# A spectral filter and a gated FFN on one core: inverse column transforms as five 64-row pairs, and an FFN begun on two of four token tiles

## The chip, the cores and the metric

The kernel runs on one core of a Trainium2 chip. A core has a matrix engine (PE, with its weight loads shown apart as PEld), VectorE (DVE), ScalarE (ACT), GpSimd (POOL) and SyncE (SP), which here only issues DMAs. Each engine works off its own queue in order; they meet through semaphores. The metric is device time in microseconds for one execution, as the median of several runs. The profile is of one further execution and has its own time.

## The reference

```python
def _A_ref(x, w_r, w_i):
    X = jnp.fft.rfft2(x.astype(jnp.float32), axes=(-2, -1))
    X = X * (w_r + 1j * w_i)
    return jnp.fft.irfft2(X, s=(S, D), axes=(-2, -1)).astype(jnp.bfloat16)

def _B_ref(x, w_gate, w_up, w_down):
    return (gelu(x @ w_gate) * (x @ w_up)) @ w_down

h   = x + _A_ref(layernorm(x), w_r, w_i)
out = h + _B_ref(layernorm(h), w_gate, w_up, w_down)
```

S is 2048 tokens, D is 576, the FFN is F = 4608 wide; inputs are bfloat16. A is a two-dimensional Fourier transform over tokens and features, a product with a complex weight, and the inverse. B is a feed-forward block with a gate (Gelu by the tanh formula).

## The kernel before, in words

The Fourier transforms are matmuls with tables of sines and cosines that the kernel makes itself. A token index is split into 16 x 128, so that a transform over tokens is one of length 16 (F16, `row16`, line 288) followed by one of length 128 with twiddles in the tables TF (forward) and TI (inverse, TF turned by a DMA transpose, `turn_tf`, line 261). The feature transform uses the table DT (three blocks of 128 features), with DF, DI and DS as rearranged pieces of it: DI and DS are filled by six small DMAs (lines 413 to 421). Only J = 289 of the 576 feature frequencies are kept.

The middle part (lines 646 to 685) is a hand-made pipeline over eight column groups, in the order 1, 2, ..., 7, 0. For group k:

- `f2` (line 471): 6 matmuls per column, two columns (k and k + 8), 290 wide; the result `pq` is copied from PSUM by ACT (VectorE for column 9).
- `f3` (line 496): two halves of 4 matmuls; ACT copies the results `g` and `hs`.
- `sums_of` (line 520): VectorE forms `xab` from g and hs, two operations.
- `wmul` (line 526): VectorE multiplies with the filter's parts (WR, WI; `m1`, `m2`), forms `za`, `zb`, and writes the two halves of Zt (lines 552 and 553). That makes eight VectorE operations a group with the two of the next group's `sums_of`, which stand between zb and Zt. Group 0 is written in two pieces of its columns.
- `i3` (line 557): the inverse of the length-128 transform, 10 matmuls 256 wide (24 of 128 for group 0), in three steps spread between other matmuls; ACT copies the results into EO.

Three Zt buffers go round. `weights()` (line 451) writes the negated second half of WI and halves the first and last column of WR and WI, on VectorE, before the first group's multiplication.

Then come the inverse column transforms, `inv_cols(x, g)` (line 613), for two halves x of the groups and eight g of 256 tokens: six matmuls of 128 rows, 290 wide, three for the even and three for the odd frequencies, each half into a PSUM bank of its own. ACT copies the result (scaled) to `cw` or `cs`. `add_rows` and `add_sum` (lines 731 and 782) do the length-16 inverse on PE and add the result to h, with the sum over features; ACT forms the sum of squares, `head_rstd` (line 792) makes mean and 1/deviation on VectorE with a power on POOL.

The normalised rows must lie with features on partitions for the FFN. Two ways: `norm2` writes the row with each 64 features doubled and `flip` turns it by a DMA transpose on SP's queue; `norm_row` and `turn` let PE turn it (18 transposes of 64 columns) and VectorE or ACT copy it. Of the first four token tiles 0 and 1 go by DMA and 2 and 3 by PE. The order of this head is written out by hand in lines 821 to 847.

The FFN (lines 863 to 929) takes four chunks of 512 tokens. For each of 36 blocks of 128 FFN columns PE does 18 matmuls of 64 rows, 512 wide (line 876): the upper 64 partitions hold the gate's weights, the lower the up-projection's, so that pairs run side by side into two banks. ACT does the Gelu (line 884), VectorE the product (line 885). Weights come in groups of three blocks (`load_gu`, line 141), three buffers. Then W_down: 15 token tiles with pairs of 64 rows (line 897), the last one with 128 rows (line 916). The row sums for later tiles, their norms and flips are put between blocks by the table `todo`. All PSUM tiles of two banks share a ring of four (tag `two`).

Of the kernel before, what the change touches and what calls it, by code (L numbers as in the profile page):

```python
# [32 lines left out]
NJT = 3  # L33
ZS = 320
# [7 lines left out]
def kernel_body(  # L42
# [64 lines left out]
    DI = keep.tile([P, 2, 2, JH], BF16, name="DI")  # L107
    DS = keep.tile([P, 2, 2, JH], BF16, name="DS")
# [54 lines left out]
    Zts = [sp.tile([P, 4, ZS], BF16, name=f"Zt{i}") for i in range(3)]  # L163
# [235 lines left out]
    G.memset(DI[:], 0.0)  # L399
    for z in Zts:  # L400
        G.memset(z[:, :, J:], 0.0)
# [9 lines left out]
    nc.sync.dma_start(WR[:, 9 : H + 1, 0:J], wm[0][:].rearrange("p (r j) -> p r j", r=8))  # L411
    turn_tf(first)
    for dst, src in (
        (DI[64:128, :, 1, :], DT[0:64, 0, :, 1, :]),
        (DI[0 : J - 2 * P, :, 0, :], D3[0 : J - 2 * P, :, 0, :]),
        (DS[0:64, 0, :, :], DT[64:128, 0, :, 1, :]),
        (DS[64:128, 0, :, :], DT[0:64, 1, :, 1, :]),
        (DS[0:64, 1, :, :], DT[64:128, 1, :, 1, :]),
        (DS[64:128, 1, :, :], D3[0:64, :, 1, :]),
    ):  # L420
        nc.sync.dma_start(dst, src)
# [29 lines left out]
    def weights():  # L451
        V.tensor_scalar(WI[:, 9 : H + 1, 0:J], wm[1][:].rearrange("p (r j) -> p r j", r=8), -1.0, None, op0=ALU.mult)
        for w in (WR, WI):
            V.tensor_scalar(w[:, :, 0 : J : J - 1], w[:, :, 0 : J : J - 1], 0.5, None, op0=ALU.mult)
# [5 lines left out]
    pq = {}  # L460
    xab = {}
# [9 lines left out]
    def f2(c):  # L471
# [5 lines left out]
        for par, t in steps:  # L477
# [7 lines left out]
        sb = wk.tile([P, 2, JP], BF16, name="pq", tag="pq", bufs=6)  # L485
        (V.tensor_copy if c == 9 else A.copy)(  # L486
            sb[:].rearrange("p r (j a) -> p r j a", a=2),
            ps[:, :, 0:JP].rearrange("p a (r j) -> p r j a", r=2),
        )
        pq[c] = sb  # L490
# [5 lines left out]
    def f3(k, half):  # L496
# [12 lines left out]
        for r in range(2):  # L509
            if half:  # L510
                comb(ps[:, 1 - r, 0:J], k, C, q[:, r, 0:J], NS, p[:, r, 0:J])
            else:
                comb(ps[:, r, 0:J], k, C, p[:, r, 0:J], SN, q[:, r, 0:J])
# [11 lines left out]

    def wmul(k, i, nxt=None):
        x = xab[k]
        z = Zts[i % 3]
        zt[k] = z
        zv = z[:].rearrange("p (a b) j -> p a b j", a=2)  # L530
        sl = slice(k, 18 - k, 17 - 2 * k) if k else slice(0, 9, 8)
        m1, m2 = (wk.tile([P, 2, 2, JP], BF16, name=n, tag=n, bufs=1) for n in ("m1", "m2"))
        if k:
            za, zb = (wk.tile([P, 2, JP], BF16, name=n, tag=n, bufs=1) for n in ("za", "zb"))
        else:
            za, zb = zv[:, 0], zv[:, 1]

        for j0, j1 in ((0, J),) if k else ((0, P), (P, J)):
            js = slice(j0, j1)
            for w, m in ((WR, m1), (WI, m2)):  # L540
                V.tensor_tensor(
                    m[:, :, :, js],
                    x[:, :, :, js],
                    w[:, sl, js].unsqueeze(1).to_broadcast([P, 2, 2, j1 - j0]),
                    ALU.mult,
                )
            V.tensor_tensor(za[:, :, js], m1[:, 0, :, js], m2[:, 1, :, js], ALU.subtract)
            V.tensor_tensor(zb[:, :, js], m1[:, 1, :, js], m2[:, 0, :, js], ALU.add)
            if nxt:
                sums_of(nxt)  # L550
            if k:
                V.tensor_tensor(zv[:, 0, :, js], za[:, :, js], zb[:, ::-1, js], ALU.add)
                V.tensor_tensor(zv[:, 1, :, js], zb[:, :, js], za[:, ::-1, js], ALU.subtract)
# [3 lines left out]
    def i3(k, s):  # L557
# [3 lines left out]
        z = zt[k][:].rearrange("p c j -> p (c j)")  # L561
# [3 lines left out]
        if k:  # L565
            pv = ps[:].rearrange("p a (n h e l) -> p (a n) e h l", n=2, h=H, l=8)
            for n, w in (((0, 0), (1, 1)), ((2, 3), (3, 4)), ((0, 2),))[s]:
                o = w * P
                T.matmul(pv[:, n], lhsT=z[:, o : o + P], rhs=TI[:, ts[k], 1:3, :], start=True, stop=False)  # L569
                o += 2 * ZS  # L570
                T.matmul(pv[:, n], lhsT=z[:, o : o + P], rhs=TI[:, ts[k], 0:2, :], start=False, stop=True)  # L571
# [13 lines left out]
        for n, c, j, p0, m in (  # L585
            ((0, 0, 0, 0, P), (1, 0, P, 0, P)),
            ((0, 1, 64, 0, P), (1, 1, 192, 0, P)),
            ((0, 0, 256, 0, 64), (0, 1, 0, 64, 64)),
        )[s]:
            for b in range(2):  # L590
                for a in range(2):
                    T.matmul(
                        pv[p0 : p0 + m, n, b],
                        lhsT=z[:, (2 * a + b) * ZS + j : (2 * a + b) * ZS + j + m],
                        rhs=TI[:, ts[8 * b], 1 - a + c, :],
                        start=(a == 0),
                        stop=(a == 1),
                    )
# [14 lines left out]
    def inv_cols(x, g):  # L613

        ps = two("cs_ps")
        for e in range(2):
# [30 lines left out]
    for i in range(n + 1):  # L647
        last = i >= n
        if not last:
            f2(order[i])  # L650
# [325 lines left out]
```

## Time and profile before

| | us |
|---|---|
| median of 3 runs | 502.45 |
| lowest and highest | 502.14, 502.9 |
| the profiled execution, its own time | 502.53 |
| its span in the trace | 500.8 |
| PE busy in the span | 490.8 |

The span runs from the first to the last instruction of the program; the profiled execution's own time has 1.73 us around it. In a group's row the columns are: line, engine, operation, output <- input, shapes, count, then busy time in us, mean ns of one, and the idle time of the engine before them. In a timeline row the columns are start and length in us, engine, line, operation, tiles, shapes, count, and in brackets the idle time before it with what ended it; lengths overlap the next start, so steps are read from start to start. A row of the chain has start, length, engine, tile, line and count. A row of a window has the stretch, its length, the busy time of PE, PEld, DVE, ACT and POOL, the granted PE clock, the DMA share and GB/s. DMA rows end with the size and the time from issue to landing.

### The profile page before, as it was taken

To read this page: it belongs to the slowest core of one execution; us is meant where nothing else is said; L and a number is where in the kernel's file an instruction comes from. 1 tells how busy PE (TensorE), PEld (TensorE's weight loads), DVE (VectorE), ACT (ScalarE), POOL (GpSimd) and SP (SyncE) were. 2 spreads that over 40 slices of the span, in tenths; PEclk is the share of its full clock that TensorE was granted. 3 is DMA by queue.
4 is the path that set the end of the run, shared out by engine and by line. 5 is a ranking of instruction groups with operands and counts; after the bars stand their busy time and mean duration, and the time that the engine had idled before them with its cause. 6 is when DMAs were issued, how large, how long until landed. Compare 5 with 4: busy or idle time off the path is not lost.

```text
span 500.8 us, 12115 instructions
## 1 busy us (share of the span) xinstructions
PE 490.8 (98%) x5418; PEld 316.9 (63%) x5420; DVE 222.9 (45%) x435; ACT 162.3 (32%) x284; POOL 28.5 (6%) x75
## 2 busy tenths in 40 slices
PE   7999999999999999999999999999999999999997
PEld 3467765555569974444499944444799644445995
DVE  8999766788641234433321154333212233333111
ACT  8989973322220112232300123232110223233000
POOL 8500010111110000000000000000000000000000
PEclk9999999999999999999999999999999999999999
DMA  8539686799950029998810099998400497880000
GB/s 282 167 75 200 172 236 160 153 171 193 177 109 3 1 76 192 198 196 156 159 22 1 3 189 189 198 183 156 82 1 3 112 186 154 155 155 1 14 14 24
DMA packets 88114, 61.61 MB, mean 123 GB/s; under 512 B 22781, under 2 KB 86653, under 8 KB 88061
## 3 DMA queue, kind: packets, MB, share of 16 engines
q1 hardware_dynamic: 87773, 59.65, 60.5%
q0 software_dynamic: 288, 1.18, 0.7%
q8 instruction: 42, 0.69, 0.6%
q14 instruction: 11, 0.09, 0.1%
HBM read 52.65 MB, written 2.36 MB: 110 GB/s over the span
## 4 chain that ended last, share of the span: by engine, by line
PE 92%; DVE 3%; ACT 2%; DMA 1%; POOL 1%; issue 0%; POOLq 0%
PE gu L876 56%; PE acc L897 26%; PE pq_ps L478 2%; PE acc L916 2%; PE cs_ps L618 1%; PE f2t L286 1%; PE eo_ps L571 1%; PE y_ps L741 1%; PE eo_ps L569 1%; DMA Bt<-hrow 1%; PE gh_ps L494 1%; ACT Bt L322 1%; DMA h_sb<-in_A_x_dram 1%; DVE h_sb L786 1%; PE gh_ps L493 1%; ACT junk L124 1%
## 5 line engine op out<-in xcount | busy, mean ns | idle before, releaser
L876 PE MATMUL gu<-Bt,wgu 64*128 64x512 bf16 x2592 | 282.2, 376 | 0.9 <-DMA Bt<-hrow 0.9
L876 PEld LDWEIGHTS <-wgu 64*128 64x128 bf16 x2592 | 132.7, 94 | 146.8 <-issue 1.2
L885 DVE TENSOR_TENSOR P_sb<-g_sb,gu 128x512 bf16<-128x512 f32 x144 | 98.7, 685 | 148.8 <-ACT g_sb L884 148.8
L884 ACT ACTIVATE g_sb<-gu 128x512 f32<-128x512 f32 x144 | 86.0, 597 | 196.8 <-PE gu L876 196.8
L897 PEld LDWEIGHTS <-P_sb 64*128 64x128 bf16 x2160 | 130.0, 94 | 3.3
L897 PE MATMUL acc<-wd,P_sb 64*128 64x288 bf16 x1440 | 93.0, 283 | 0.0
L906 DVE TENSOR_TENSOR part<-part,acc 128x576 f32<-128x576 f32 x15 | 11.3, 754 | 111.4 <-ACT part L905 111.4
L905 ACT COPY part<-acc 128x576 f32<-128x576 f32 x15 | 9.6, 638 | 122.5 <-PE acc L897 122.5
L897 PE MATMUL acc<-wd_a,P_sb 64*128 64x288 bf16 x720 | 48.9, 283 | 0.0
L478 PE MATMUL pq_ps<-DT,Bt 128*128 128x290 bf16 x64 | 12.2, 287 | 0.2 <-DVE Bt L328 0.2
L286 PE MATMUL f2t<-h_sb,ident 128*128 128x512 bf16 x26 | 8.8, 494 | 3.7 <-DMA h_sb<-in_A_x_dram 3.7
L766 DVE TENSOR_SCALAR hrow<-h_sb,mv,rstd 128x1152 bf16<-128x1152 bf16 x14 | 12.1, 866 | 0.0
L908 DVE TENSOR_TENSOR h_sb<-h_sb,part 128x576 bf16<-128x576 bf16 x15 | 11.4, 757 | 0.5
L134 POOL TENSOR_TENSOR rstd<-rstd,mhalf 128x1 f32<-128x1 f32 (+1 forms) x16 | 11.2, 699 | 1.3
L618 PEld LDWEIGHTS <-EO 128*128 128x128 bf16 x96 | 9.1, 96 | 3.0 <-issue 0.2
L478 PEld LDWEIGHTS <-Bt 128*128 128x128 bf16 x96 | 9.3, 97 | 2.5 <-issue 0.2
L298 PE MATMUL f2t<-F,xn 128*128 128x256 bf16 x64 | 9.2, 275 | 1.1 <-DVE xn L137 1.0
L133 POOL TENSOR_SCALAR rstd<-mv 128x1 f32<-128x1 f32 (+1 forms) x16 | 3.9, 244 | 107.1 <-DVE mv L119 106.9
L486 ACT CAST pq<-pq_ps 128x580 bf16<-128x580 f32 x15 | 9.8, 662 | 0.4 <-PE pq_ps L478 0.2
L124 ACT ACTIVATE junk<-h_sb 128x576 bf16<-128x576 bf16 x14 | 9.4, 677 | 0.4 <-DMA h_sb<-in_A_x_dram 0.4
L118 DVE BATCH_NORM_STATS2 st<-h_sb 128x6 f32<-128x288 bf16 x21 | 9.3, 442 | 0.0
L117 DVE BATCH_NORM_STATS2 st<-h_sb 128x6 f32<-128x288 bf16 x21 | 9.3, 441 | 0.0
(137 smaller groups left out, 283.5 us busy)
## 6 DMA issues: line engine op xcount, KB each, us to landing
wgu<-in_B_w_gate_dram SPq DMA_DIRECT2D x48, 432.0 KB, 5.3
wgu<-in_B_w_up_dram SPq DMA_DIRECT2D x48, 432.0 KB, 6.9
wd<-in_B_w_down_dram SPq DMA_DIRECT2D x2, 1728.0 KB, 7.7
wd_a<-in_B_w_down_dram SPq DMA_DIRECT2D x1, 1728.0 KB, 15.1
out_dram<-h_sb SPq DMA_DIRECT2D x3, 576.0 KB, 3.9
h_sb<-in_A_x_dram SPq DMA_DIRECT2D x4, 288.0 KB, 3.2
h_sb<-in_A_x_dram SPq DMA_DIRECT2D x2, 576.0 KB, 6.6
WR<-in_A_w_r_dram SPq DMA_DIRECT2D x1, 650.2 KB, 8.8
```

The lines of the kernel that those rows point to most:

```text
L124: A.activation(junk[:], h_sb[:, h, :], fn, scale=sc, accum_out=mv[:, h, i : i + 1])
L134: G.tensor_tensor(dst[:, sl], dst[:, sl], mhalf[:, sl], ALU.pow)
L286: T.matmul(dst, lhsT=ident[:], rhs=h_sb[:, 0, 0:512], start=True, stop=True)
L478: T.matmul(ps[:, par, 0:JP], lhsT=Bt[:, t, col], rhs=DT[:, t // 2, par] if t < 4 else DF[:, par], start=(t == par), stop=(t == 4),)
L618: T.matmul(ps[:, e, 0:JP], lhsT=EO[x][:, 2 * e + jt if jt < 2 else 4, 2 * g : 2 * g + 2].rearrange("p h e k l -> p (h e k l)"), rhs=DI[:, ...
L766: V.tensor_scalar(hrow[:], h_sb[:, h, :].rearrange("p (r k) -> p r k", k=64).unsqueeze(2).to_broadcast([P, NR, 2, 64]), mv2[:, h, 0:1], rs ...
L876: T.matmul(gu[:, c, :], lhsT=w[rows, r, i * P : (i + 1) * P], rhs=hl[tcnk % 2][rows, r, :], start=(r == 0), stop=(r == NR - 1),)
L884: A.activation(g_sb[:], gu[:, 0, :], ACT.Gelu_apprx_tanh)
L885: V.tensor_tensor(p_sb(fa + i), g_sb[:], gu[:, 1, :], ALU.mult)
L897: T.matmul(accs[i][:, c, 0:DH], lhsT=p_sb(f)[rows, st * P : (st + 1) * P], rhs=wd[f // NWA][rows, f % NWA, c * DH : (c + 1) * DH], start=( ...
L906: V.tensor_tensor(part[:], part[:], accs[1][:, :, 0:DH], ALU.add)
L908: V.tensor_tensor(hv, hv, part[:], ALU.add)
```

## The change

Six parts.

1. `inv_cols` takes the 290 frequencies in five blocks of 58 (JW, NW). Even ones lie on partitions 0 to 57, odd ones on 64 to 121, so that ten matmuls of 58 rows make five pairs, one on each half of PE's rows. The table for it is DQ, filled by 13 small DMAs, in place of DI and DS. Zt gets the layout [2, 5, 2, 64] with 58 of 64 used.
2. `f3` gives both outputs of its first half from the first half of pq, and of its second half from the second. Column 9's copy is made in two pieces. The copy of the second group's first column comes after `f3` of the first.
3. WI's second half comes by DMA, without the sign; the halving of two columns is done by POOL; `weights()` is gone. m1 and m2 are allocated once.
4. The second half of Zt is held back and written in the next group's `wmul`, between the second multiplication and za (for the last groups at once). i3's three steps stand together at the end of a turn. Group 0's i3 has 40 matmuls of 64 columns.
5. In the head, tiles 0 and 1 go by PE and tiles 2 and 3 by DMA; VectorE does both copies. Two of the second half's transforms that stood ahead of the FFN stay there, beside the first two; the last four go between FFN blocks.
6. The FFN's first six blocks are done in two sweeps: first for 256 tokens (tiles 0 and 1), with a late transform behind each of the second to the fifth block, then for the other 256. Weight groups are requested when their buffer's last block has been issued. `part` shares a buffer tag with `g_sb`.

```diff
-NJT = 3
-ZS = 320
+JW = 58
+NW = JP // JW
...
+    DQ = keep.tile([P, NW, 2, JH], BF16, name="DQ")
+    Zts = [sp.tile([P, 2, NW, 2, 64], BF16, name=f"Zt{i}") for i in range(3)]
...
-    nc.sync.dma_start(WR[:, 9 : H + 1, 0:J], wm[0][:].rearrange("p (r j) -> p r j", r=8))
+    for w, t in ((WR, wm[0]), (WI, wm[1])):
+        nc.sync.dma_start(w[:, 9 : H + 1, 0:J], t[:].rearrange("p (r j) -> p r j", r=8))
+    for w in (WR, WI):
+        G.tensor_scalar(w[:, :, 0 : J : J - 1], w[:, :, 0 : J : J - 1], 0.5, None, op0=ALU.mult)
     turn_tf(first)
-    for dst, src in (
...
-        nc.sync.dma_start(dst, src)
+    for r in (1, 0):
+        for w in range(1 - r, NW):
+            j0, j1 = w * JW, (w + 1) * JW
+            for lo, hi in ((j0, min(j1, (j0 // P + 1) * P)), ((j0 // P + 1) * P, j1)):
+                if lo < hi:
+                    p0 = 64 * r + lo - j0
+                    nc.sync.dma_start(
+                        DQ[p0 : p0 + hi - lo, w], DT[lo % P : lo % P + hi - lo, lo // P, :, r, :]
+                    )
...
+    m1, m2 = (wk.tile([P, 2, 2, JP], BF16, name=n) for n in ("m1", "m2"))
+    for m in (m1, m2):
+        G.memset(m[:, :, :, J:], 0.0)
...
+        r = half
+        comb(ps[:, r, 0:J], k, C, p[:, r, 0:J], SN, q[:, r, 0:J])
+        comb(ps[:, 1 - r, 0:J], k, C, q[:, r, 0:J], NS, p[:, r, 0:J])
...
         if k:
+            times(WR, m1, slice(0, J))
+            times(WI, m2, slice(0, J))
+            release()
+            za, zb = (wk.tile([P, 2, JP], BF16, name=n, tag=n, bufs=2) for n in ("za", "zb"))
+            parts(za[:], zb[:], slice(0, JP))
             if nxt:
                 sums_of(nxt)
+            V.tensor_tensor(zv[:, :, 0], blocks(za[:]), blocks(zb[:, ::-1]), ALU.add)
+            held.append((zv[:, :, 1], blocks(zb[:]), blocks(za[:, ::-1]), ALU.subtract))
+            if k in order[5:7]:
+                release()
+            return
...
     def inv_cols(x, g):
         ps = two("cs_ps")
-        for e in range(2):
-            for jt in range(NJT):
+        for w in range(NW):
+            for e in range(2):
+                rows = slice(64 * e, 64 * e + JW)
                 T.matmul(
                     ps[:, e, 0:JP],
+                    lhsT=EO[x][rows, w, 2 * g : 2 * g + 2].rearrange("p h e k l -> p (h e k l)"),
+                    rhs=DQ[rows, w] if w or e else DT[rows, 0, :, 0, :],
+                    start=(w == 0),
+                    stop=(w == NW - 1),
                 )
...
-        if last:
-            inv_cols(0, 0)
         if 1 <= i <= n:
             f3(order[i - 1], 0)
-        if i >= 3 and not last:
-            i3(order[i - 3], 0)
...
         if not last and i:
             f2(order[i] + 8)
+            f2_out(order[i] + 8)
         if i >= 3:
-            for jt in range(0 if last else 2, NJT):
-                i3(order[i - 3], jt)
+            for s in range(3):
+                i3(order[i - 3], s)
...
-    for g in (1, 2):
+    for g in (0, 1, 2):
         inv_cols(0, g)
...
     inv_cols(0, 6)
     add_sum(2, y1)
+    inv_cols(0, 7)
     head_rstd(0)
     add_sum(3, y1)
     head_rstd(1)
+    norm_row(0)
+    norm_row(1)
+    inv_cols(1, 2)
+    inv_cols(1, 3)
+    turn(0)
+    turn(1)
     head_rstd(2)
+    norm2(2)
+    flip(2)
     head_rstd(3)
+    norm2(3)
+    flip(3)
     load_wd(2)
...
+    late = [(1, g) for g in range(4, 8)]
+    for f in range(2 * FQ):
+        gate(0, f, groups[f // FQ], f % FQ, 0, 2 * P)
+        if f and late:
+            inv_cols(*late.pop(0))
     for tcnk in range(4):
         for gi in range(NG):
             for i in range(FQ):
+                f = gi * FQ + i
+                gate(tcnk, f, groups[0], i, 2 * P if tcnk == 0 and f < 2 * FQ else 0, 4 * P)
...
+            groups.pop(0)
+            n = tcnk * NG + gi + 3
+            if n < 4 * NG:
+                groups.append(load_gu(n))
```

`gate(tcnk, f, w, i, lo, hi)` is the FFN block of before for the tokens from lo to hi: 18 matmuls hi - lo wide, Gelu, product.

More of the change, by code (lines that the diff above doesn't have):

```diff
@@ L484, in f2, with f2_out @@
             )
[L485 to L488, printed above, removed]
+        pq[c] = wk.tile([P, 2, JP], BF16, name="pq", tag="pq", bufs=6)
+        pq_ps[c] = ps
+    def f2_out(c, copy=A.copy, rs=slice(0, 2)):
+        copy(
+            pq[c][:, rs].rearrange("p r (j a) -> p r j a", a=2),
+            pq_ps[c][:, :, 0:JP].rearrange("p a (r j) -> p r j a", r=2)[:, rs],
         )
-        pq[c] = sb
     def comb(dst, k1, t0, a, t1, b):
@@ L524, in sums_of, with release @@
         V.tensor_tensor(x[:, 1, ::-1, 0:J], g[:, :, 0:J], hs[:, :, 0:J], ALU.add)
+    held = []
+    def release():
+        while held:
+            V.tensor_tensor(*held.pop())
     def wmul(k, i, nxt=None):
@@ L555, in kernel_body @@
+        for w0, w1 in ((0, 2), (2, NW)):
+            lo, hi = w0 * JW, w1 * JW
+            times(WR, m1, slice(lo, min(hi, J)))
+            times(WI, m2, slice(lo, min(hi, J)))
+            V.tensor_tensor(
+                zv[:, 0, :, w0:w1], blocks(m1[:, 0, :, lo:hi]), blocks(m2[:, 1, :, lo:hi]), ALU.subtract
+            )
+            V.tensor_tensor(
+                zv[:, 1, :, w0:w1], blocks(m1[:, 1, :, lo:hi]), blocks(m2[:, 0, :, lo:hi]), ALU.add
+            )
     eo = {}
@@ L788, in add_sum, with sum_squares @@
         )
+        if squares:
+            sum_squares(h)
+    def sum_squares(h):
         junk = roll.tile([P, D], BF16, name="junk", tag="junk", bufs=2)
```

176 lines of the change are left out of this document (63 added, 113 removed).

## The prediction

> **What bounds the kernel now.** I read the page first, then busy time by window, then the chain that ended last.
>
> ```profile
> span 500.8 us, 12115 instructions
> PE 490.8 (98%) x5418; PEld 316.9 (63%) x5420; DVE 222.9 (45%) x435; ACT 162.3 (32%) x284; POOL 28.5 (6%) x75
> PE 92%; DVE 3%; ACT 2%; DMA 1%; POOL 1%; issue 0%; POOLq 0%
> ```
>
> ```profile
> 60.00:80.00 20.00, 19.04 (x204) 12.57 (x202) 11.91 (x36) 13.18 (x26) 2.14 (x4) 1.00 0.75 209
> ```
>
> ```profile
> 50.78 0.74 PE pq_ps L478 x6
> ...
> 52.61 0.12 PE gh_ps L494
> ...
> 53.49 0.11 PE eo_ps L569
> ...
> 57.34 1.49 PE cs_ps L618 x12
> 58.83 1.25 PE eo_ps L592 x24
> ...
> 62.43 1.19 PE y_ps L741 x16
> ...
> 69.50 3.41 DMA Bt<-hrow
> ...
> 73.05 9.89 PE gu L876 x90
> 82.94 0.49 PE y_ps L741 x8
> 83.43 11.65 PE gu L876 x108
> ```
>
> PE is 98% busy, so a gain must come from matmul time removed or from a wait of PE. From 73.05 on PE does nothing but FFN and row sums; the change leaves that stretch alone, except that four transforms enter it. So the whole answer lies before 78.9 us, where three FFN blocks are done (108 matmuls take 11.65, so 54 take 5.83). The chain names the last wait: 3.41 us of DMA transpose ahead of the first FFN block. But window 60 to 80 has PE busy 19.04 of 20: PE has other work there, eight column transforms. Less waiting for the DMA gains only what cannot be refilled.
>
> Ahead of that, the loop over eight column groups is paced by VectorE:
>
> ```profile
> 38.09 0.76 DVE L541 TENSOR_TENSOR m<-xab,WR 128x1156 bf16<-128x1156 bf16 x1
> 38.76 0.76 DVE L541 TENSOR_TENSOR m<-xab,WI 128x1156 bf16<-128x1156 bf16 x1
> 39.56 0.47 DVE L547 TENSOR_TENSOR za<-m,m 128x578 bf16<-128x578 bf16 x1
> ...
> 41.79 0.76 DVE L541 TENSOR_TENSOR m<-xab,WR 128x1156 bf16<-128x1156 bf16 x1
> ...
> 58.48 0.33 DVE L548 TENSOR_TENSOR Zt<-m,m 128x322 bf16<-128x322 bf16 x1
> ```
>
> Same line to same line, 38.09 to 41.79, is 3.70 us. PE's work for one group is 12 f2 matmuls (2 x 0.74), 8 of f3 at 0.12 and 10 of i3 at 0.11: 3.54. VectorE leads by 0.16, no more. Its second multiply starts 0.67 after the first, but L547, which needs that multiply's result, 0.80 after it: 0.13 of dependence.
>
> **Part A: up to the first row sum (before: 63.60).**
>
> Column transforms. Six matmuls of 128 rows cost 0.745 (1.49 for twelve). Ten of 64 rows run as five pairs; eight such matmuls of nearly this width took 0.49 (82.94), so ten take 0.61. That is 0.13 off each of 16, 2.1 in all, but only those on PE's path count. Three lie behind the last Zt write (58.48 + 0.33 = 58.81) and ahead of the row sums at 62.43: 0.4. Those ahead of it only fill time in which PE would otherwise wait for Zt. Those behind the row sums belong to part B.
>
> VectorE's eight operations per group stay, in another order: the held second Zt write now stands between the second multiply and za, and covers the 0.13. It does so in five groups of seven (the first has nothing held, the last nothing either): 0.65. PE's 3.54 lets the period fall just so far. The price is a later second half of Zt: group k's is written in the next group's turn, some 1.7 into it. i3 waits for it, with the next f2 and f3 queued behind it on PE; but i3 has moved to the end of PE's turn, behind 2.5 of f2 and f3, and VectorE wants that f3 a turn later. I cost it at nothing; uncovered, it can take back the 0.16 per group by which VectorE leads.
>
> The Zt writes get 10 runs of 58 elements for 2 of 289. Bounds:
>
> ```profile
> L766 DVE TENSOR_SCALAR hrow<-h_sb,mv,rstd 128x1152 bf16<-128x1152 bf16 x14 | 12.1, 866 | 0.0
> ```
>
> ```profile
> L541 DVE TENSOR_TENSOR m<-xab,WR 128x1156 bf16<-128x1156 bf16 x7 | 5.3, 760 | 0.0
> L541 DVE TENSOR_TENSOR m<-xab,WR 128x512 bf16<-128x512 bf16 x1 | 0.4, 419 | 0.0
> ```
>
> Four runs of 128 cost no more per element than four of 289 (341 ns for 644 more elements): nothing per run. But 18 runs of 64 in L766 took 106 ns more than L541 for the same count: 6 ns a run, 0.06 a write. I take 0.02, nearer the tensor_tensor rows: 14 writes, +0.3 (0 to +0.84).
>
> The first sums may come a little earlier:
>
> ```profile
> 29.13 0.65 ACT L514 CAST hs<-gh_ps 128x578 bf16<-128x578 f32 x1
> ```
>
> They start when this ends, at 29.8. ACT now copies the next group's pq behind g and hs, but f3's first half still needs the same two copies. I take 0.1 (0 to 0.65, one ACT copy). VectorE's `weights` (0.9) falls away ahead of that, where VectorE would wait for hs: nothing. i3 of group 0 becomes 40 matmuls of 64 columns in 20 pairs. Transposes of that width:
>
> ```profile
> 69.77 0.29 PE L618 MATMUL cs_ps<-DI,EO 128*128 128x290 bf16 x1
> 69.98 1.20 PE L811 MATMUL pt<-ident,hflat 128*64 128x128 bf16 x36
> ```
>
> 18 pairs in 1.20, of which 0.2 is the last one's tail: 0.055 a pair, 1.1 for 20, against 1.25 before. I take 0.1. These rows also show a step of 0.21 from a 128 by 128 matmul to a 128 by 64 one, where L618 repeats every 0.12: 0.09 for the change of shape. The Trainium skill ("TensorEngine Tiling (Array Packing)", Key Properties) says that a change of tiling mode drains the engine; the step agrees, and it speaks against this change, since 64-row transforms now stand between 128-row i3. I count seven such changes both before and after: behind the last Zt write two fewer, ahead of it more, where PE waits anyway.
>
> Off the path: SP issues 13 small copies for DQ instead of 6, and WI as a copy; POOL halves two weight columns and waits for that copy.
>
> ```profile
> 12.71 0.96 POOL L381 DMA_INDIRECT wm_i<-in_A_w_i_dram,rev  x1 [0.30 <-issue]
> ```
>
> ```profile
> 26.44 2.60 SPq L421 DMA_DIRECT2D DS<-DT  x4
> ...
> 33.27 3.18 SPq L262 DMA_TRANSPOSE TI<-TF  x1
> ```
>
> ```profile
> WR<-wm_r SPq DMA_DIRECT2D x1, 578.0 KB, 4.5
> wm_i<-in_A_w_i_dram,rev POOLq DMA_INDIRECT x1, 5.7
> ```
>
> WI: 12.71 + 5.7 + 4.5 = 22.9, halved by 24, wanted by VectorE at 30.7 (38.09 less two periods); queued behind it on POOL are only two memsets with the same date. SP: a copy takes 0.65 to issue, and behind the last at 29.04 the queue stood free until 33.27. Seven more end at 33.6, so the second TI transpose, queued behind, starts 0.3 late; its 3.18 end near 36.8, and its tables are first wanted by the third group's i3, near 42. The weight loads behind it are wanted at 69. All nothing; uncovered, each costs its overshoot.
>
> Sum of A: -0.1 - 0.65 + 0.3 - 0.4 - 0.1 = **-0.95**.
>
> **Part B: from the first row sum to three FFN blocks done.** Before: 73.05 + 5.83 - 63.60 = 15.28. After, offsets from that row sum:
>
> ```profile
> 63.60 0.76 DVE L786 SCALAR_TENSOR_TENSOR h_sb<-y_ps,h_sb 128x576 bf16<-128x576 f32 x1
> ...
> 66.70 0.21 DVE L795 SCALAR_TENSOR_TENSOR mv<-sums 128x1 f32<-128x1 f32 x1
> ```
>
> ```profile
> 67.17 0.55 POOL L800 TENSOR_TENSOR rstd<-rstd,mhalf 128x1 f32<-128x1 f32 x1 [0.50 <-DVE mv L799]
> ```
>
> ```profile
> L137 DVE TENSOR_SCALAR hflat<-h_sb,mv,rstd 128x576 bf16<-128x576 bf16 x2 | 0.8, 422 | 0.0
> L812 DVE COPY Bt<-pt 128x1152 bf16<-128x1152 bf16 x1 | 0.8, 757 | 0.6 <-PE pt L811 0.6
> ```
>
> The power for tile 1 ends at +4.12, norm_row(1) at +4.6, 18 transposes with their tail at +5.4, the copy at +6.2: the first block starts at **+6.25**, not +9.45. What is late next, with the DMA gone, is this chain of VectorE and POOL: in those 6.25 PE has four transforms (2.45), 36 transposes (1.2) and the rest of the row sums, and idles some 2. That is what the early start costs. Then six half blocks, 5.83. With 256 columns a 64-row pair isn't in the trace; i3's 128-row matmuls of 256 columns step by 0.11, so +0.14 in all (0 if by columns; 0.12 a pair, as for 288, gives +1.6). Four transforms: 2.45.
>
> ```profile
> L885 DVE TENSOR_TENSOR P_sb<-g_sb,gu 128x512 bf16<-128x512 f32 x144 | 98.7, 685 | 148.8 <-ACT g_sb L884 148.8
> ```
>
> One new wait: VectorE does norm2 of tiles 2 and 3 (two scalings 0.37, powers 0.55, norms 0.87) ahead of the first gate product, which ends near +10.2 (half of L885). The second late transform takes the first block's PSUM buffer (four in the ring) and PE is there at +9.8: +0.4; all later matmuls queue behind. Total 6.25 + 5.83 + 0.14 + 2.45 + 0.4 = 15.07: **-0.2**.
>
> Cover: tile 3's hrow is ready at +9.85 and lands 3.5 later, +13.4; wanted at +15.07. The weights:
>
> ```profile
> wgu<-in_B_w_gate_dram SPq DMA_DIRECT2D x48, 432.0 KB, 5.3
> wgu<-in_B_w_up_dram SPq DMA_DIRECT2D x48, 432.0 KB, 6.9
> wd<-in_B_w_down_dram SPq DMA_DIRECT2D x2, 1728.0 KB, 7.7
> ```
>
> Group 0 is freed only after its second halves, +18; the next group lands at +18 + 0.7 + 6.9 = +25.6, wanted at +26.7. W_down's second part, issued behind the flips (+11.3), lands at +19 and overlaps by one: the cover is 0 to 1 us.
>
> Late transforms put a scaled ACT copy between Gelus, which this trace doesn't have.
>
> ```profile
> L884 ACT ACT_TABLE_LOAD x1 | 1.3, 1283 | 0.0
> ```
>
> I cost it at nothing: copies and squares ran under the sine's table with no load. The Trainium skill ("ScalarE: Activation LUTs", Table sets) says that copy is in every set; no run here shows it for Gelu's.
>
> **Total** -0.95 - 0.2 = -1.15. The profiled execution took 502.53 (span 500.8), the median is 502.45: **501.3**.
>
> **Rivals.**
> - *All free* (10%): short runs cost nothing, no PSUM wait, the 0.14 gone: 500.5. The L541 rows speak for it.
> - *The gain is eaten* (23%): runs at 0.06 a write (+0.55), or the fourth weight group up to 1 us late: 502.1. L766 and the thin cover speak for it.
> - *Slower: 58-element runs fall to one element a cycle* (11%). L541's 644 extra elements in 341 ns are two per cycle; at half that rate a write of 580 costs +0.3, 14 writes and group 0's four +4.6, all on VectorE's chain: 505.9. It decides from +0.15 a write. L766, with runs of 64, stays well above that rate, which speaks against. The Trainium skill ("Vector Engine (DVE) Microarchitecture Reference", 5.2) keeps the full rate for runs of two or more adjacent words; by it the forecast stands.
> - *The pairs don't pair* (6%, with the table loads): slices of 58 rows, not 64, run one by one; a transform costs 1.23, some +8. All pairs in the trace have 64 rows.
>
> **Chances.** Forecast 50% (500.8 to 501.8). 0.2%, or 1.0 us, is what a measurement tells from no change: 501.45 is the border, and the forecast lies just beyond it. Faster: 10% and 33 of the 50; same: 17 and the 23; slower: 17. Range 500.3 to 503.0: it takes in the eaten gain and pairs at 0.12, and leaves out the slower cases.
>
> **What would show it.** First gu near 68.9 and PE idle about 2 us before it; VectorE's period 3.57 to 3.6; transforms 0.61; the first row sum at 62.6; a PE wait of about 0.4 in the half blocks; no wait on wgu. Wrong if Zt writes take 0.7, if the half blocks' pairs step by 0.12, or if ACT loads tables between Gelus.

## The result, and the profile after

The changed kernel took **501.08 us** (median of 9 runs, 500.86 to 501.75), the kernel before beside it 502.57 (9 runs, 502.14 to 502.90). The ratio is 0.9973, with a 95% interval of 0.9965 to 0.9982: faster by 1.4 us, where 1.15 were forecast. The profiled execution took 500.97, of which 499.1 is the span. In the page of the profile after, and in its window from 60 to 80:

```profile
span 499.1 us, 12531 instructions
PE 488.1 (98%) x5606; PEld 341.8 (68%) x5608; DVE 222.4 (45%) x439; ACT 162.7 (33%) x289; POOL 29.0 (6%) x78
```

```profile
60.00:80.00 20.00, 18.32 (x319) 16.24 (x317) 11.85 (x35) 13.55 (x28) 2.41 (x4) 1.00 0.73 194
```

PE is still busy 98% of the span. Between 60 and 80 it is busy 18.32 where it was 19.04: the changed kernel waits more in its head, not less, and yet ends earlier. The chain of the profile after, around the head:

```profile
57.73 1.24 PE eo_ps L616 x40
58.97 0.75 PE cs_ps L643 x10
...
62.26 2.11 DVE h_sb L809 x6
...
65.82 0.74 POOL rstd L827
...
67.07 0.71 PE pt L836 x18
67.80 0.76 DVE Bt L837
...
72.19 0.42 DVE P_sb L899
...
72.65 0.80 PE cs_ps L643 x10
73.45 0.98 PE gu L890 x18
74.43 0.63 PE cs_ps L643 x10
...
76.67 5.90 PE gu L890 x108
```

The DMA transpose is gone from the chain. In its place stand the power on POOL, 18 transposes, VectorE's copy, and then VectorE's first product, for which a late transform waits. A transform steps by 0.63 (74.43 to 75.06, the next gu) and a half block takes 0.98. Stages, by the traces' starts in us (the first row sum is `h_sb`'s first, "three blocks" the end of as many gu matmuls as three full blocks have):

| | before | after | difference |
|---|---|---|---|
| first `xab` on VectorE | 29.82 | 29.21 | -0.61 |
| last `gh_ps` matmul (end of the loop on PE) | 53.20 | 51.71 | -1.49, of it -0.88 in the loop |
| last Zt write on VectorE | 58.48 | 57.46 | -1.02 |
| first row sum | 63.60 | 62.25 | -1.35, of it +0.14 behind the loop |
| first gu | 73.05 | 68.71 | -4.34 |
| three blocks done | 78.88 | 77.47 | -1.41, of it -0.06 behind the row sum |
| end of the span | 500.8 | 499.1 | -1.7, of it -0.3 behind the three blocks |

By these stages the gain shows in three places: the start, the loop and the FFN. The start on two tiles, which moves first gu by 4.34, is not among them. Of the 0.88 in the loop, 0.75 is one transform that the kernel before has ahead of its last `gh_ps` and the changed kernel has behind it. So stages don't say what each part of the change is worth; the runs below put parts back one at a time.

### The profile page after: what moved, and what is told of

It is laid out like the page before. It is cut to its first block, busy times and chain, and to the rows that moved or that the text cites. A ratio compares the mean times of both kernels' runs of the same rounds, so it can differ in the third digit from the quotient of the medians.

```text
span 499.1 us, 12531 instructions
## 1 busy us (share of the span) xinstructions
PE 488.1 (98%) x5606; PEld 341.8 (68%) x5608; DVE 222.4 (45%) x439; ACT 162.7 (33%) x289; POOL 29.0 (6%) x78
## 4 chain that ended last, share of the span: by engine, by line
PE 90%; DVE 2%; ACT 1%; POOL 0%; issue 0%
PE gu L890 55%; PE acc L926 27%; PE acc L945 2%; PE eo_ps L592 2%; PE cs_ps L643 1%; PE pq_ps L478 1%; PE y_ps L764 1%; DVE h_sb L809 1%; PE gh_ps L495 0%; PE gh_ps L496 0%; POOL rstd L827 0%; PE eo_ps L616 0%; DVE hrow L789 0%; DVE Bt L837 0%; PE pt L836 0%
## 5 line engine op out<-in xcount | busy, mean ns | idle before, releaser
L890 PE MATMUL gu<-Bt,wgu 64*128 64x512 bf16 (+1 forms) x2700 | 282.4, 367 | 0.9 <-DVE mv L822 0.9
L890 PEld LDWEIGHTS <-wgu 64*128 64x128 bf16 x2700 | 159.6, 94 | 119.7 <-issue 1.1
L899 DVE TENSOR_TENSOR P_sb<-g_sb,gu 128x512 bf16<-128x512 f32 (+1 forms) x150 | 99.4, 664 | 146.0 <-ACT g_sb L898 146.0
L898 ACT ACTIVATE g_sb<-gu 128x512 f32<-128x512 f32 (+1 forms) x150 | 87.0, 580 | 194.6 <-PE gu L890 194.6
L926 PEld LDWEIGHTS <-P_sb 64*128 64x128 bf16 x2160 | 128.5, 94 | 4.5
L926 PE MATMUL acc<-wd,P_sb 64*128 64x288 bf16 x1440 | 91.0, 283 | 0.0
L926 PE MATMUL acc<-wd_a,P_sb 64*128 64x288 bf16 x720 | 46.9, 283 | 0.0
L643 PE MATMUL cs_ps<-DQ,EO 58*128 58x290 bf16 x144 | 11.6, 283 | 0.0
L643 PEld LDWEIGHTS <-EO 58*128 58x128 bf16 x160 | 8.2, 94 | 2.8 <-issue 1.1
L117 DVE BATCH_NORM_STATS2 st<-h_sb 128x6 f32<-128x288 bf16 x21 | 9.3, 442 | 0.0
```

The lines of the kernel that those rows point to most:

```text
L643: T.matmul(ps[:, e, 0:JP], lhsT=EO[x][rows, w, 2 * g : 2 * g + 2].rearrange("p h e k l -> p (h e k l)"), rhs=DQ[rows, w] if w or e else DT ...
L890: T.matmul(gu[:, c, 0:n], lhsT=w[rows, r, i * P : (i + 1) * P], rhs=hl[tcnk % 2][rows, r, lo:hi], start=(r == 0), stop=(r == NR - 1),)
L898: A.activation(g_sb, gu[:, 0, 0:n], ACT.Gelu_apprx_tanh)
L899: V.tensor_tensor(p_sb(f)[:, lo:hi], g_sb, gu[:, 1, 0:n], ALU.mult)
L926: T.matmul(accs[i][:, c, 0:DH], lhsT=p_sb(f)[rows, st * P : (st + 1) * P], rhs=wd[f // NWA][rows, f % NWA, c * DH : (c + 1) * DH], start=( ...
```

## Experiments

Theory at the start: the gain is the sum of about 0.5 at 21 us (a POOL memset that stood beside a VectorE normalise is gone), 0.4 in the loop (the held Zt write), 0.35 by paired transforms, 0.06 by the start on two tiles and 0.25 by weights requested earlier. Rivals: the first and the last are chance; the loop is bound by PE; the start on two tiles is what pays.

**Marks.** The changed kernel ran with the experiments twice. First:

> The changed kernel itself, as the mark for the other runs. Both theories: 1.3 to 1.7 us below the kernel before (ratio 0.9965 to 0.9975), first gu near 68.7 us of the span.

501.11, ratio to the kernel before 0.9974 (0.9964 to 0.9984). And later:

> The changed kernel once more, as the mark beside e10_six_pairs on the same chip: 1.3 to 1.7 us below the kernel before.

500.93, 0.9976 (0.9966 to 0.9985). The profiles differ by 0.24 already at first pq_ps (25.27 in the first, 25.03 in the second and in the profile after): so much is chance of the start. It is there already ahead of the last four normalises on VectorE, which start at 21.07 in the first mark, as in the kernel before, and at 20.89 in the profile after.

**The memset put back** (`e1_memset_back`).

```diff
+    DI = keep.tile([P, 2, 2, JH], BF16, name="DI")
+    G.memset(DI[:], 0.0)
     for z in Zts:
```

> The DI tile and its memset on GpSimd are put back ahead of the Zt memsets; nothing uses the tile. Theory: the 0.5 us that the changed kernel gained before its first pq_ps came from VectorE's first normalise (945 ns before, 505 ns after), which the DI memset on GpSimd stood beside; so the normalise takes 800 ns or more again, the first pq_ps starts near 25.4 instead of 25.03, and the time is 0.3 to 0.6 us above the changed kernel. Rival: the 0.5 us is the chance of one execution's early timing; the first pq_ps stays near 25.0 and the time is within 0.2 us of the changed kernel.

Four normalises of VectorE and what POOL did beside them, in timeline rows: of the kernel before,

```profile
21.07 1.96 DVE L137 TENSOR_SCALAR xn<-h_sb,mv,rstd 128x576 bf16<-128x576 bf16 x4 [0.28 <-POOL rstd L134]
```

```profile
21.00 0.57 POOL L399 MEMSET DI<- 128x580 bf16 x1
21.52 0.63 POOL L401 MEMSET Zt<- 128x124 bf16 x3
```

of the changed kernel, in the profile after and in the first mark,

```profile
20.89 1.52 DVE L136 TENSOR_SCALAR xn<-h_sb,mv,rstd 128x576 bf16<-128x576 bf16 x4
```

```profile
21.07 1.57 DVE L136 TENSOR_SCALAR xn<-h_sb,mv,rstd 128x576 bf16<-128x576 bf16 x4 [0.28 <-POOL rstd L133]
```

and with the memset back:

```profile
20.97 1.73 DVE L136 TENSOR_SCALAR xn<-h_sb,mv,rstd 128x576 bf16<-128x576 bf16 x4
```

```profile
20.68 0.75 POOL L399 MEMSET DI<- 128x580 bf16 x1
```

The same four operations take 1.96 with the memset in the kernel before, 1.52 and 1.57 without it, and 1.73 with it put back: in these rows the overlap with POOL's memset goes with longer operations, by 0.2 to 0.4. What decides the size is not shown. First pq_ps came at 25.21, 0.18 behind the profile after, but 0.06 ahead of the first mark, so that this trace alone doesn't tell the memset from the chance of the start. The first mark beside the kernel before does better, since both start the four at 21.07: first pq_ps comes at 25.27 and at 25.53. So about 0.26 of the 0.5 goes with the memset and 0.24 with the start.

The time was 501.61, ratio 0.9980 (0.9971 to 0.9988), 0.5 above the mark, though the intervals overlap. The eleven runs fall into two groups: four from 501.04 to 501.14, where most of the mark's runs lie, and seven from 501.48 to 502.12; of all 27 runs of the changed kernel (9, 8 and 10) only three lie above 501.16. So the direction is the theory's, and most runs show more than the trace, which is that of the lowest run (501.04).

**The second Zt write not held** (`e3_not_held`).

```diff
-            if k in order[5:7]:
-                release()
+            release()
```

> The second Zt write is no longer held back to the next group's turn, but made at once for every group, as in the kernel before; all else stays as changed. Theory: VectorE's dependence bubble of 0.13 us comes back in five groups, its period goes from 3.58 to about 3.70, the last Zt write ends 0.4 to 0.6 us later (near 58.3) and the time rises by 0.4 to 0.6 us. Rival: the loop is bound by PE's 3.54 a group, whatever VectorE does; the period stays at 3.58 to 3.60 and the time within 0.2 us of the changed kernel.

VectorE's rows of the changed kernel, then of this one:

```profile
40.71 0.76 DVE L543 TENSOR_TENSOR m<-xab,WR 128x1156 bf16<-128x1156 bf16 x1
41.39 0.76 DVE L543 TENSOR_TENSOR m<-xab,WI 128x1156 bf16<-128x1156 bf16 x1
42.06 0.45 DVE L530 TENSOR_TENSOR Zt<-zb,za 128x580 bf16<-128x580 bf16 x1
42.43 0.45 DVE L548 TENSOR_TENSOR za<-m,m 128x580 bf16<-128x580 bf16 x1
...
44.28 0.76 DVE L543 TENSOR_TENSOR m<-xab,WR 128x1156 bf16<-128x1156 bf16 x1
```

```profile
41.31 0.76 DVE L543 TENSOR_TENSOR m<-xab,WR 128x1156 bf16<-128x1156 bf16 x1
41.98 0.76 DVE L543 TENSOR_TENSOR m<-xab,WI 128x1156 bf16<-128x1156 bf16 x1
42.78 0.46 DVE L548 TENSOR_TENSOR za<-m,m 128x580 bf16<-128x580 bf16 x1
...
45.01 0.76 DVE L543 TENSOR_TENSOR m<-xab,WR 128x1156 bf16<-128x1156 bf16 x1
```

From multiply to multiply it is 3.57 with the write held (40.71 to 44.28) and 3.70 without. The reader sees why: unheld, za starts 0.80 behind the second multiply; held, the Zt write starts after 0.67 and za 0.37 later, with no gap. On PE it shows at the i3 behind the last f3, held and unheld:

```profile
51.94 1.26 PE L592 MATMUL eo_ps<-TI,Zt 128*128 128x256 bf16 x10
```

```profile
52.55 1.27 PE L591 MATMUL eo_ps<-TI,Zt 128*128 128x256 bf16 x10 [0.86 <-DVE Zt L530]
```

Unheld, PE waits 0.86 for Zt there and starts 0.61 later; the first row sum came 0.61 later too (62.86). (The last `gh_ps` stands at 51.40 unheld and at 51.71 held, so that mark of the stages is not the price of the loop.) The time was 501.65, ratio 0.9984 (0.9975 to 0.9993), 0.54 above the mark. The theory holds. With the write held, the chain of the profile after is PE's alone from 35.45 to 59.72, so there VectorE hardly sets the pace any more.

**The old head** (`e4_old_head`): tiles 0 and 1 by DMA, all transforms ahead of the FFN, no half blocks.

```diff
...
-    late = [(1, g) for g in range(4, 8)]
-    for f in range(2 * FQ):
-        gate(0, f, groups[f // FQ], f % FQ, 0, 2 * P)
...
-                gate(tcnk, f, groups[0], i, 2 * P if tcnk == 0 and f < 2 * FQ else 0, 4 * P)
+                gate(tcnk, f, groups[0], i, 0, 4 * P)
```

> The head of the FFN is put back: the order of the row sums, the two tiles turned by DMA first and the two turned by PE last, all sixteen column transforms ahead of the FFN, no half blocks. The paired transforms, the held Zt write and the loop stay as changed. Theory: the start on two tiles is worth almost nothing, since what it starts early it pays in idle PE ahead of it and in half blocks; the time rises by 0 to 0.3 us, while first gu moves from 68.7 to about 71.7. Rival: the early start is what the change gains by; without it the time is that of the kernel before, 1.4 us above the changed kernel.

The time was 502.98, ratio 1.0014 (1.0002 to 1.0026), in two groups of six runs: 501.94 to 502.30 and 503.67 to 504.51. Even the lower is 1.0 above the mark. First gu came at 72.80, only 0.25 earlier than in the kernel before, though the first row sum came 1.33 earlier (62.27). The theory's 0 to 0.3 fell. Its chain, and two rows of the DMA queues between 68.1 and 72.7 with the rates in 40 slices:

```profile
68.05 0.11 DVE hflat L136
68.16 4.50 DMA Bt<-hrow
```

```profile
GB/s 223 216 209 203 227 203 205 169 203 181 78 127 227 207 220 203 354 211 200 189 96 65 18 4 0 7 7 11 9 9 9 11 198 281 386 411 381 190 260 341
...
q8 instruction: 1, 0.02, 1.4%
```

A transpose took 4.50 where the kernel before had 3.41. The rates fall to 0 to 18 GB/s for ten slices of 0.115 us. The hole begins 0.7 behind the start (69.95) of one packet of q8, the DMA queue that brings the engines' instructions; such a packet has 16 KB. In the kernel before the same stretch (69.4 to 72.95) has no such packet and no such hole. The packets go by the count of PE's instructions, matmuls and weight loads together: this trace has 43 packets for 10998, one for 256 on average (210 to 310 from one to the next between 38 and 110 us). They are called code fetches here. So a new theory: a code fetch that falls into a DMA transpose stalls it, and the old head loses 1.1 by it and nothing else.

**The old head, code fetches moved** (`e8_old_head_shifted`).

```diff
-        for _ in range(n):
-            T.matmul(dst, lhsT=ident[:], rhs=h_sb[:, 0, 0:512], start=True, stop=True)
+        for _ in range(4 * n):
+            T.matmul(dst[:, 0:128], lhsT=ident[:], rhs=h_sb[:, 0, 0:128], start=True, stop=True)
```

> The old head as in e4_old_head; beside it, TensorE's 27 filler matmuls of 512 columns in the first 21 us are 108 of 128 columns, the same columns in four times the instructions, so that every later code fetch of TensorE (one 16 KB packet per 220 to 300 of its instructions) comes some 160 instructions earlier. In e4_old_head such a fetch, at 69.98, stood inside the second DMA transpose, whose packets nearly stopped from 70.6 to 71.8; in the kernel before, at 67.18, it stood ahead of both. New theory (the early start did not pay by itself; it took the first blocks off a transpose that a code fetch can stall): no 16 KB fetch between 67.8 and 71.5, the transpose lands near 71.4, first gu starts near 71.6 and the time falls by 1.0 to 1.2 us below the faster half of e4_old_head, to within 0.3 us of the changed kernel (501.1). Rival (a transpose issued 1.3 us earlier takes 1.1 us longer for another reason, and the early start pays 1.0 by itself): first gu stays near 72.8, the time near 502.1.

```profile
68.89 3.47 DMA Bt<-hrow
```

With no instruction packet between 68.8 and 72.4 the transpose took 3.47. The fillers made the start 0.74 later in this profile (first row sum 63.00), so first gu came at 72.50, not at 71.6; but from the row sum it is 9.50 in place of 10.54. The time was 501.11 (500.82 to 501.65; the profile is of the highest run), ratio 0.9969 (0.9958 to 0.9981), and the upper group is gone. The new theory holds; the rival fell. The request for W_down, which SP issues next, does not set the traces apart: it follows the first transpose by 2.85 to 2.92 in the kernel before, here, in `e4_old_head` and in `e9_before_shifted`, with the hole and without.

**The kernel before, code fetches moved** (`e9_before_shifted`): the same edit on the kernel before.

> The kernel before with the filler edit of e8_old_head_shifted alone (108 matmuls of 128 columns for 27 of 512), the test from the other side. The 16 KB code fetch that stood at 78.07 moves some 160 TensorE instructions ahead, to between 69.5 and 72, into the DMA transposes that it had missed (they ran from 69.0 to 72.5). The fillers themselves cost up to 0.75, as in e8_old_head_shifted. Theory (a code fetch stalls a transpose): from the first row sum to first gu 10.3 to 10.8 us in place of 9.45, the time 1.5 to 2 us above the kernel before. Rival (fetches are harmless, the transpose of e4_old_head was long for another reason): 9.4 to 9.6 us, the time 0.5 to 0.8 us above.

```profile
69.10 4.93 DMA Bt<-hrow
```

```profile
GB/s 217 213 213 199 215 215 167 190 193 92 142 213 213 217 336 211 201 201 111 25 6 0 0 0 0 0 6 6 10 8 10 10 13 255 291 365 395 348 160 329
...
q8 instruction: 1, 0.02, 1.9%
```

These rates are of 69.1 to 74.0, 0.12 a slice. The fetch came at 70.9, the hole is there, the transpose takes 4.93, first gu comes 10.97 behind the row sum in place of 9.45, a little more than expected, and the time was 503.88 (502.88 to 505.40), 1.5 above the kernel before beside it: ratio 1.0032 (1.0019 to 1.0044). Shown from both sides: the kernel before had missed the fetch by luck. Why a fetch holds up a transpose, these traces don't tell.

**Transforms with no pair next to each other** (`e5_unpaired`).

```diff
-        for w in range(NW):
-            for e in range(2):
+        for e in range(2):
+            for w in range(NW):
```

> The changed kernel with the ten matmuls of a column transform in another order: the five of the upper 64 rows first, then the five of the lower, so that no two neighbours can run beside each other. Theory: a transform takes 1.15 to 1.25 us in place of 0.62; the loop's transforms fill waits of TensorE, some twelve others lie on its path, so the time rises by 5 to 8 us. Rival: TensorE runs matmuls of different row halves side by side whatever their order; a transform stays at 0.62 and the time within 0.3 us of the changed kernel.

501.41, ratio 0.9980 (0.9970 to 0.9990): 0.3 above the mark. The theory of 5 to 8 us fell. Against the first mark, whose first pq_ps is the same (25.27 and 25.26), the first row sum comes 0.42 later and the span is 0.6 longer (499.9 and 499.3), so the order is not quite free. Timeline rows of PE:

```profile
59.40 0.29 PE L643 MATMUL cs_ps<-DT,EO 58*128 58x290 bf16 x1
59.54 0.68 PE L643 MATMUL cs_ps<-DQ,EO 58*128 58x290 bf16 x8
60.04 0.28 PE L643 MATMUL cs_ps<-DT,EO 58*128 58x290 bf16 x1
60.06 0.78 PE L643 MATMUL cs_ps<-DQ,EO 58*128 58x290 bf16 x9
60.66 0.28 PE L643 MATMUL cs_ps<-DT,EO 58*128 58x290 bf16 x1
```

DT is the first matmul of a transform. In the changed kernel a second one starts beside it; here the next starts 0.14 later, and eight follow ahead of the next DT, 0.64 after the first. Then the steps are 0.62, as with neighbours paired. The five lower ones, five places further in the program, ran beside the upper ones; only the first transform of a row pays some 0.12, which over three rows ahead of the row sum makes most of the 0.42. What in TensorE lets them run so, these traces don't tell.

**Six pairs for five** (`e10_six_pairs`): each transform's first pair is done twice, the result is the same.

```diff
-        for w in range(NW):
+        for i, w in enumerate((0, *range(NW))):
...
-                    stop=(w == NW - 1),
+                    stop=(i == 0 or w == NW - 1),
```

> The changed kernel with its first pair of 64-row matmuls done twice in every column transform, the second time over the first: six pairs, 0.745 us a transform again, as long as the six 128-row matmuls of the kernel before. Theory: of 16 transforms only those on TensorE's path count, three behind the last Zt write (0.37) and four among the half blocks (0.5); the time rises by 0.7 to 1.0 us, with 0.3 to 0.4 of it ahead of the first row sum. Rival: the transforms still only fill waits, at most 0.2 us; or all 16 count, 2.0 us.

```profile
59.58 2.35 PE cs_ps L643 x34
61.93 0.37 PE y_ps L764 x6
...
74.43 0.98 PE gu L890 x18
75.41 0.75 PE cs_ps L643 x12
```

A transform takes 0.75 (75.41 to 76.16). The first row sum came at 63.11, 0.86 later, three blocks were done 15.59 behind it (after: 15.22). The time was 502.10, beside 500.93 of the mark and 502.10 of the kernel before: ratio 1.000 (0.9991 to 1.0009). **Put back into the changed kernel, the longer transforms cost 1.17 us, as much as the whole gain beside them.** That is above the 0.7 to 1.0 expected and below the 2.0 of all 16. Ahead of the row sum not three of them count but all eight behind the loop: PE's first row-sum matmul moves from 60.78 to 61.76, 0.98 or eight times 0.12. The first row sum itself moves by 0.12 less, since in the changed kernel the chain ahead of it leaves PE for copies of ACT and VectorE (59.74 to 61.44) and in this run it does not.

**The kernel before with early weight requests** (`e2_before_early_load`).

```diff
-            n = tcnk * NG + gi + 2
-            if 3 <= n < 4 * NG:
-                groups.append(load_gu(n))
...
+            n = tcnk * NG + gi + 3
+            if n < 4 * NG:
+                groups.append(load_gu(n))
```

> The kernel before with one edit: the next group of FFN weights is requested at the end of a group's turn, as in the changed kernel, and no longer at the start of the next one. Theory: the one stall of TensorE in the FFN, at the first block of the second chunk (192.65 us, 0.43 us in the kernel before), goes, and the time falls by 0.2 to 0.4 us below the kernel before. Rival: the stall is chance; the time is within 0.15 us of the kernel before.

The waits of PE's weight loads in the kernel before, 185 to 196 us, and SP's requests there:

```profile
PEld L876 <- DMA wgu<-in_B_w_up_dram: 0.5, 1, 0.5
```

```profile
184.20 0.62 SPq L145 DMA_DIRECT2D wgu<-in_B_w_gate_dram  x1
...
189.60 4.47 SPq L778 DMA_TRANSPOSE Bt<-hrow  x1
```

With the edit one group is requested at 146.13, ahead of W_down, the row at 184.20 is gone, and so is the wait. The span was 500.4 in place of 500.8, the time 501.86, ratio 0.9989 (0.9980 to 0.9998): 0.6 below the kernel before, by the interval 0.1 to 1.0. Theory in direction and place; the time a little more than the 0.3 of the trace.

**Another order in the head** (`e6_head_order`).

```diff
     add_sum(2, y1)
     inv_cols(0, 7)
-    add_sum(3, y1)
     head_rstd(0)
     head_rstd(1)
+    add_sum(3, y1)
...
+    head_rstd(2)
     turn(0)
     turn(1)
-    head_rstd(2)
+    head_rstd(3)
     norm2(2)
     flip(2)
-    head_rstd(3)
```

> The changed kernel with VectorE's small operations in the head in another order: the statistics of tiles 0 and 1 ahead of the last row sum, those of tiles 2 and 3 one tile ahead of the norms that need them. Theory: the power on GpSimd for tile 1 no longer waits for the row sum of tile 3, first gu starts 0.3 to 0.5 us earlier (near 68.3), the wait of 0.38 in the half blocks for VectorE goes, and the time is 0.4 to 0.8 us below the changed kernel (500.3 to 500.7). Rival: TensorE has no other work there, so what the first block gains is given back as waits in the half blocks; the time within 0.2 us of the changed kernel.

500.50 (500.28 to 500.53), ratio 0.9960 (0.9946 to 0.9973). In its chain:

```profile
68.49 2.14 PE gu L890 x36
70.63 0.63 PE cs_ps L643 x10
71.26 0.98 PE gu L890 x18
```

First gu came at 68.49, 0.22 earlier than in the changed kernel (0.3 to 0.5 were expected). PE waits no more from the first block on, where the changed kernel lost 0.38; three blocks were done at 76.89, 0.58 earlier. The theory holds, with less of it ahead of first gu than it said. This version is ahead of both kernels.

**The same with the Zt memsets later** (`e7_memsets_later`).

```diff
-    for z in Zts:
-        G.memset(z[:].rearrange("p a w b j -> p (a w b) j")[:, :, JW:], 0.0)
...
-    for w in (WR, WI):
+    for w in (WI, WR):
         G.tensor_scalar(w[:, :, 0 : J : J - 1], w[:, :, 0 : J : J - 1], 0.5, None, op0=ALU.mult)
+    for z in Zts:
+        G.memset(z[:].rearrange("p a w b j -> p (a w b) j")[:, :, JW:], 0.0)
```

> e6_head_order with the memsets of Zt on GpSimd moved behind the halving of the weight columns, away from VectorE's last normalises. Theory: the first of these normalises takes 410 to 430 ns in place of 505 to 555, first pq_ps starts 0.1 to 0.2 us earlier, and the time is 0.1 to 0.2 us below e6_head_order (near 500.35). Rival: the same wait moves to the halving, which then stands beside the normalises; the time within 0.1 us of e6_head_order or above it.

500.42, ratio 0.9965 (0.9952 to 0.9978): no difference from `e6_head_order`, as its rival had it.

```profile
20.89 1.45 DVE L136 TENSOR_SCALAR xn<-h_sb,mv,rstd 128x576 bf16<-128x576 bf16 x4
```

The four normalises fell from 1.52 to 1.45, but first pq_ps stayed at 25.03: 0.07 less on VectorE was not on the path.

## Why the prediction was right, and where its steps were not

The time is 0.2 from the forecast, and its two parts have the right sign. Its terms are less good. On one side it missed gains at the start, in the transforms and in the FFN, and charged the short runs too much; on the other it missed what changes of shape cost and expected more of the two tiles. These errors cancel in large part, and so far the closeness of the total is luck.

- **The start, -0.1.** It was -0.61. Behind first pq_ps it was -0.11, as costed. The other 0.5 was not foreseen: the prediction doesn't name the DI memset that the change removes, and puts POOL off the path without asking what it does to VectorE beside it. About 0.26 of the 0.5 goes with the memset (`a0_after` beside the kernel before), the rest is the chance of a start.
- **The held write, -0.65.** Right: 0.61 when undone, with a period of 3.57 (3.57 to 3.6 was said). That leaves no room for a price of i3's later half, which was put at nothing.
- **Runs of 58, +0.3.** They cost nothing: a Zt write of ten runs takes 455 ns, where one of two runs took 460. The bound of nothing was the value, but not for the reason given: L541's two rows have four runs each (of 128 and of 289), so their difference can't show what a run costs. The Trainium skill ("Vector Engine (DVE) Microarchitecture Reference", 5.2), by which runs of two or more adjacent words keep the full rate, agrees with the 455 and 460.

```profile
L562 DVE TENSOR_TENSOR Zt<-za,zb 128x580 bf16<-128x580 bf16 x7 | 3.2, 455 | 0.1
```

```profile
L552 DVE TENSOR_TENSOR Zt<-za,zb 128x578 bf16<-128x578 bf16 x7 | 3.2, 460 | 0.1
```

- **Three transforms on the path, -0.4.** The step "Those ahead of it only fill time in which PE would otherwise wait for Zt" failed. A transform took 0.62 as forecast, but from 51.94 on the changed kernel's PE has no wait left to fill: all eight behind the loop move PE, and 0.86 of that reaches the first row sum (`e10_six_pairs`). In the kernel before there was still such a wait, at 56.19 in its chain and among the waits of PE's weight loads from 53.2 to 63.6:

```profile
56.19 0.28 PE eo_ps L571
```

```profile
PEld L571 <- DVE Zt L553: 0.3, 1, 0.3
```

The Zt write waited for ended at 56.13 (55.67 + 0.46). The same write ends at 55.04 in the changed kernel (54.58 + 0.46): the earlier start and the held write took away the wait that the transforms were to fill. Behind 56.19 the chain of the kernel before is PE's without a wait up to the row sums, so two of the five transforms ahead of the last Zt write stood on PE's chain even there.
- **The modes.** The step that shape changes ahead of the last Zt write fall "where PE waits anyway" failed for the same reason. Four steps behind the loop are about 0.1 longer than their matmuls (ten i3 of 0.109 from 51.94 end at 53.03, but the transform starts at 53.13), some 0.4 in all; the kernel before has no such gap between i3 and a transform (ten i3 from 53.33, the transform at 54.42). It is not a wait for Zt: in `e10_six_pairs` PE comes to two of these i3 later by 0.37 and 0.61, and the same 0.24 stands ahead of their weight loads. Also, the change moves one more transform, 0.62, from the loop to behind it. That is why this stretch is 0.14 longer than before in spite of the pairs, and the loop 0.88 shorter.
- **i3 of group 0, -0.1.** Right: 1.24 for 1.34 (58.67 to 60.01 before, 57.66 to 58.90 after).
- **First gu at +6.25.** It came at +6.46, with PE idle 0.94 just ahead of it and 1.36 in all behind the row sum, where some 2 were said. The wait of 0.4 for VectorE's product was there, 0.38 (72.27 to 72.65). Half blocks take 0.98, so nine pairs step by 0.109, as for i3. No table load stood between the Gelus, so the Trainium skill ("ScalarE: Activation LUTs", Table sets) agrees here. The part came to 15.22 where 15.07 was said: -0.06, not -0.2.
- **The start on two tiles as such** is worth 0.11 against the old head where no code fetch falls into its transpose (`e8_old_head_shifted`: 15.33 from the row sum to three blocks), and 1.15 where one does (`e4_old_head`: 16.37). The prediction took the 3.41 of one profile as a constant of the old head.
- **"From 73.05 on ... the change leaves that stretch alone"** failed. The early request of weights removes a wait of 0.5 on wgu at 192 us, which the waits of the kernel before show. The prediction looked at the first weight groups only, where none is. That is 0.3 of the span behind the three blocks.

Terms put back one by one (1.17, 0.54, 0.3 to 0.6, about 0.26 and 0.1) come to some 1.0 more than the 1.4 gained. The shape changes take some 0.4 of that. The rest is not divided by any run: a term put back into the changed kernel is priced where PE is the limit, and in the kernel before the limit was still VectorE up to 56.19. No run has the shorter transforms without the held write. Also open are the upper groups of times in `e4_old_head` and `e9_before_shifted`, which no profile caught, and how much of the 0.5 at the start lasts over many runs.

## What to carry to other kernels

Ask of each removed instruction not only whether it is on the path but what it disturbs beside it, and look through the waits of the whole kernel, not of the edited stretch alone, when a request is moved. Whether work "only fills waits" is to be read for the kernel as it will be: here another part of the same change took the waits away, and ahead of the row sums the shorter transforms were worth 0.86 in place of 0.4. A DMA duration from one profile is no constant: see which fetches it missed, and prefer an order that doesn't wait on it.

## What the runs showed of the hardware

- DMA transposes into which a code fetch fell (a 16 KB packet, one for some 256 of TensorE's instructions: 43 for 10998) took 4.50 and 4.93 us, others 3.41 and 3.47; 81 more filler matmuls at the start moved the fetches into the transpose or out of it.
- Matmuls on the two halves of TensorE's rows ran side by side though five places apart in the program (`e5_unpaired`: 0.62 a transform).
- Four normalises on VectorE took 1.45 us with no memset on GpSimd beside them, 1.52 and 1.57 beside three of 120 elements, 1.73 and 1.96 with one of 580 elements ahead of those.
- A step from a 128-row i3 to a 58-row transform, or back, was some 0.1 us longer than the matmuls alone (53.03 to 53.13 in the profile after).
